# A planner in the kernel sets the order of every engine: chunked attention, then a Fourier mix and an MLP

## The chip, the core and the metric

The kernel runs on one NeuronCore of a Trainium2 chip. The metric is the device time of one execution in microseconds (us). Five engines work side by side and meet through semaphores: PE (TensorE, matrix products, results in PSUM), DVE (VectorE), ACT (ScalarE), POOL (GpSimd) and SP, which only starts DMA transfers. Each engine runs its own list of instructions strictly in the order in which the program put them there: an instruction that has to wait holds up all that stand behind it on its engine. That order is what this change is about.

## What is computed

The reference has two parts. The first is attention in chunks over 4 batches of 8 heads with 768 positions and 64 channels: each chunk of 32 queries sees 8 memory keys, 16 positions to its left, itself and 8 positions to its right.

```
for c in range(nc):
    k_full = np.concatenate([mem_k, k_ctx], axis=2)
    v_full = np.concatenate([mem_v, v_ctx], axis=2)
    scores = scale * np.matmul(q_c, k_full.transpose(0, 1, 3, 2))
    a = np.exp(scores - np.max(scores, axis=-1, keepdims=True))
    a = a / (np.sum(a, axis=-1, keepdims=True) + 1e-09)
    out[:, :, c_start:c_end] = np.matmul(a, v_full)
```

The heads are then laid side by side, so that x has the shape 4 x 768 x 512, and the second part follows (w_ch1 is 512 x 2048, w_ch2 is 2048 x 512):

```
X = np.fft.fft(np.fft.fft(x, axis=1), axis=2)
u = x + np.real(X)
un = (u - mean(u)) / sqrt(var(u) + 1e-6)
out = u + np.maximum(un @ w_ch1, 0.0) @ w_ch2
```

## The kernel before, in words

**Attention** (`emit_keys`, `emit_pair`) works on pairs of heads, four pairs to a batch, 16 in all. For a pair, SP loads q, k and v; the casts of q and k to bf16 (L239, L241) run on DVE for batch 0 and on POOL for the others; POOL copies the overlapping rows of v (L245). PE turns q and k (trq, L250; trk, L259), ACT copies them out of PSUM (qT, L252; kTb, L264). Then there are two groups, each half of the positions: PE computes the scores (sc, L282), ACT the exponential (e, L287), PE the product with v (xa, L299), DVE divides by the sum and writes the activations (L303, L304). There is one PSUM buffer for scores.

**The Fourier mix** (`emit_fx`) of a batch needs all four pairs of it. DVE folds the activations (zy, pq, ff: L319 to L328) for the even part and then for the odd part. ACT rounds the fold to fp16 (hi, L332), DVE takes the rest (lo, L333), PE multiplies both with cosine and sine tables (ps, L341, L348), ACT and DVE split the result again (L355, L356, L358). Six column products follow (pm, L370), one for each tile of 128 positions; DVE adds each to the activations (L379), takes mean and variance (L381, L382) and subtracts the mean (un, L384); PE turns the result (tp, L387) and DVE copies it out (unT, L388). POOL computes the inverse deviation (L391, L392).

**The MLP** (`emit_mlp`) of a batch runs in two halves of 384 positions. A half is 16 groups of 4 matmuls (ph, L403), each followed by a relu on ACT (hT, L406), and then 3 groups of 16 matmuls (pc, L411), each followed by a scaled addition on DVE (osb, L414) and a store. The half's first products need three of the six unT tiles. There are two PSUM buffers for ph and pc together (tag `mlp`), two for the Fourier products (tag `acc`), and one hT.

The tables of cosines and sines are made at the start: DVE computes the angles (L178 to L185), ACT applies Sin (L197 to L203). The weights are loaded by eight transfers that POOL issues (L214, L218).

What sets the order: the scheduler of the framework orders the instructions of each engine, from its own cost model and from priorities. `emit_attention` and `emit_fx` of batch b+1 are emitted before `emit_mlp(b)`, which stands in `tc.high_priority(offset=-100000)`, so that MLP instructions go where the others leave room.

## Time and profile before

| | |
|---|---|
| time before, median of 3 runs | 361.38 us (358.62 to 362.24) |
| the profiled execution | 362.82 us, of which the span from first to last instruction is 360.8 us |
| PE busy | 300.4 us (83% of the span) |
| DVE busy | 196.1 us (54%) |
| ACT busy | 148.6 us (41%) |
| POOL busy | 81.4 us (23%) |

The page cuts the span into 40 equal slices of 9 us and gives for each the busy share of an engine in tenths. Lists of groups give, for one line and kind of instruction, its count, total and mean duration. The timeline gives single instructions with their start and duration; in brackets stands the idle time before and what ended it. A busy PE is not a PE at its peak, since matmuls overlap and their ends are modelled: the throughput is read from long runs of matmuls.

### The profile page before, as it was taken

Reading aid. Unit: us, or ns where it says so; the run is one execution under the profiler, and the core shown is the slowest. Engines: PE = TensorE matmul, PEld = TensorE weight load, DVE = VectorE, ACT = ScalarE, POOL = GpSimd, SP = SyncE. Lnnn points to the kernel's source line nnn. Section 1 sums busy time; section 2 is a strip of 40 time slices with the busy share of each in tenths; the row PEclk is TensorE's granted clock in tenths of the full one; section 3 lists DMA queues with packets and bytes.
Section 4 is the critical chain, followed back from the end, with each engine's and each line's share of the span. In section 5 each row is a group of like instructions: output and inputs, shape, how many; then the busy total and the mean of one; then the engine's idle time right before and its main releaser. Section 6 shows DMA issues by size and latency. Waiting matters only on the chain.

```text
span 360.8 us, 6878 instructions
## 1 busy us (share of the span) xinstructions
PE 300.4 (83%) x2848; PEld 186.3 (52%) x2848; DVE 196.1 (54%) x376; ACT 148.6 (41%) x258; POOL 81.4 (23%) x93
## 2 busy tenths in 40 slices
PE   0225661877899997999999969999999999999995
PEld 0124551656655463666554636775555566554542
DVE  8933339959712139989211398794013987901001
ACT  1654440343372466341743474415651741160530
POOL 7623431601340324020712250206000000100000
PEclk9999985589999999999999998999999999999998
DMA  7997999942000690065402680034101000001001
GB/s 130 200 174 144 189 195 238 156 97 46 6 2 31 146 180 7 32 130 142 133 18 85 161 141 0 2 102 129 25 21 70 0 2 29 37 23 56 34 17 71
DMA packets 42022, 30.65 MB, mean 85 GB/s; under 512 B 30216, under 2 KB 32264, under 8 KB 41992
## 3 DMA queue, kind: packets, MB, share of 16 engines
q1 hardware_dynamic: 35848, 19.73, 29.0%
q0 software_dynamic: 2688, 4.19, 6.6%
q10 hardware_dynamic: 3456, 6.29, 4.7%
q8 instruction: 22, 0.36, 0.5%
q14 instruction: 8, 0.07, 0.1%
HBM read 28.11 MB, written 6.29 MB: 95 GB/s over the span
## 4 chain that ended last, share of the span: by engine, by line
PE 71%; DVE 13%; ACT 8%; issue 3%; POOL 2%; DMA 2%; SPq 1%; ACTq 0%; POOLq 0%; DVEq 0%
PE pc L411 23%; PE ph L403 20%; PE xa L299 9%; PE ps L341 5%; PE pm L370 5%; ACT e L287 3%; PE sc L282 2%; DVE zy L319 2%; ACT hi L332 2%; PE tp L387 2%; PE trq L250 2%; PE trk L259 2%; DMA va<-in_v_dram 2%; DVE pq L322 1%; DVE pq L321 1%
## 5 line engine op out<-in xcount | busy, mean ns | idle before, releaser
L403 PE MATMUL ph<-unT,w_sb 128*128 128x384 f16 x512 | 96.1, 328 | 3.8 <-ACT hT L406 2.9
L411 PE MATMUL pc<-w_sb,hT 128*128 128x512 f16 x384 | 93.1, 380 | 0.0
L406 ACT ACTIVATE hT<-ph 128x384 f16<-128x384 f32 x128 | 61.9, 492 | 71.6 <-PE ph L403 57.7
L403 PEld LDWEIGHTS <-w_sb 128*128 128x128 f16 x512 | 48.1, 98 | 40.7 <-issue 12.6
L411 PEld LDWEIGHTS <-hT 128*128 128x128 f16 x384 | 35.1, 98 | 35.5 <-issue 0.5
L414 DVE SCALAR_TENSOR_TENSOR osb<-pc,rstd,xsb 128x512 f32<-128x512 f32 x24 | 17.9, 746 | 63.7 <-PE pc L411 61.7
L299 PE MATMUL xa<-va,e 128*64 128x65 f32 x768 | 41.6, 253 | 10.2 <-issue 5.3
L299 PEld LDWEIGHTS xa<-va,e 128*64 128x64 f32 x768 | 33.4, 159 | 23.2 <-issue 14.9
L287 ACT ACTIVATE e<-sc,mbias 128x384 f32<-128x384 f32 x64 | 33.7, 579 | 22.1 <-PE sc L282 21.8
L245 POOL COPY va<-va 32x780 f32<-32x780 f32 x32 | 31.0, 986 | 44.8 <-DMA va<-in_v_dram 41.1
L303 DVE RECIPROCAL zs<-xa 128x6 f32<-128x6 f32 x32 | 6.1, 190 | 62.9 <-PE xa L299 62.7
L252 ACT COPY qT<-trq 128x768 bf16<-128x768 bf16 x16 | 12.8, 798 | 51.6 <-PE trq L250 49.9
L239 POOL CAST qb<-qf 96x1024 bf16<-96x1024 f32 x12 | 13.2, 1097 | 83.8 <-PE trq L250 45.2
L341 PE MATMUL ps<-cosS,hi 128*128 128x193 f16 x48 | 11.1, 278 | 14.8 <-ACT hi L332 14.8
L391 POOL TENSOR_SCALAR rstd<-mu_s 128x6 f32<-128x6 f32 x4 | 1.7, 418 | 94.5 <-DVE mu_s L382 69.7
L282 PE MATMUL sc<-qT,kTb 64*128 64x64 bf16 x384 | 12.8, 200 | 9.4 <-ACT e L287 4.7
L332 ACT CAST hi<-ff 128x1536 f16<-128x1536 f32 x8 | 11.8, 1472 | 19.1 <-DVE ff L328 16.0
L341 PEld LDWEIGHTS <-hi 128*128 128x128 f16 x96 | 9.7, 107 | 18.3 <-ACT hi L332 17.9
L264 ACT COPY kTb<-trk 128x832 bf16<-128x832 bf16 x16 | 13.6, 850 | 13.4 <-PE trk L259 13.3
L304 DVE TENSOR_TENSOR xsb<-xa,zs 128x384 f32<-128x384 f32 x32 | 17.7, 554 | 0.8
L282 PEld LDWEIGHTS <-kTb 64*128 64x128 bf16 x384 | 8.9, 99 | 16.8 <-ACT kTb L264 8.6
L355 ACT CAST up<-ps 128x386 f16<-128x386 f32 x16 | 9.6, 599 | 18.0 <-PE ps L341 13.7
(92 smaller groups left out, 381.6 us busy)
## 6 DMA issues: line engine op xcount, KB each, us to landing
qf<-in_q_dram SPq DMA_DIRECT2D x16, 384.0 KB, 3.6
kf<-in_k_dram SPq DMA_DIRECT2D x16, 384.0 KB, 5.2
out_dram<-osb ACTq DMA_DIRECT2D x24, 256.0 KB, 2.0
va<-in_v_dram SPq DMA_DIRECT2D x32, 144.0 KB, 4.1
w_sb<-in_moe_w_ch_dram POOLq DMA_DIRECT2D x8, 512.0 KB, 13.7
va<-in_v_dram SPq DMA_DIRECT2D x32, 48.0 KB, 5.9
va<-in_mem_v_dram SPq DMA_DIRECT2D x32, 24.0 KB
mkf<-in_mem_k_dram SPq DMA_DIRECT2D x1, 64.0 KB
```

Source lines behind the costliest of these rows:

```text
L245: nc.gpsimd.tensor_copy(v1[96:128, 0:NT, 0:D + 1], v1[0:32, 1:NB, 0:D + 1])
L282: nc.tensor.matmul(sc[:, hh, t6, :], kT[r0:r0 + 64, t * BS:t * BS + P], qT[r0:r0 + 64, ts(t, 64)], start=True, stop=True, tile_position=(r ...
L287: nc.scalar.activation(e1[:, :, :, ts(half, 32)], sc[:, :, 0:6, ts(half, 32)], AFT.Exp, bias=mbias[:, half:half + 1], scale=1.0 / math.sqr ...
L299: nc.tensor.matmul(xa[64 * half:64 * half + 64, st, hh, 0:65], e1[:, hh, t6, :], v1[:, 6 * g + t6, 0:65], start=True, stop=True)
L304: nc.vector.tensor_tensor(xb[:, 3 * g:3 * g + 3, h * D:(h + 2) * D].rearrange("p s (h d) -> p s h d", h=2), xa[:, :, :, 0:D], zs.unsqueeze ...
L332: nc.scalar.copy(hi.rearrange(fl), ff.rearrange(fl))
L341: nc.tensor.matmul(ps[:, sp, :], part[:, ab, sp * 3 + st, :], tab[:, sp, st, :], start=(st == 0 and i == 0), stop=(st == 2 and i == 1))
L370: nc.tensor.matmul(pm[:, par, :], lhs, rhs[:, par, :], start=(im == 0), stop=(im == 3))
L403: nc.tensor.matmul(ph[:, 0:384], w1_sb[:, dt, ts(ht, P)], unT[:, dt, sh * 384:(sh + 1) * 384], start=(dt == 0), stop=(dt == NDT - 1))
L406: nc.scalar.activation(hT[:, ht, :], ph[:, 0:384], AFT.Relu)
L411: nc.tensor.matmul(pc, hT[:, ht, ts(stl, P)], w2_sb[:, ht, :], start=(ht == 0), stop=(ht == NHT - 1))
L414: nc.vector.scalar_tensor_tensor(osb, pc, rstd[:, st:st + 1], xb[:, st, :], ALU.mult, ALU.add)
```

## The change

The framework's scheduler is switched off (`tc.manual_schedule()`); the kernel holds a planner, `Plan`, to which every step is added as a task with its engine, a cost in us, the tasks that it needs, the buffers it takes and gives back, and a rank. `Plan.order` goes through time; whenever an engine is idle in the plan, the first task of lowest rank goes next whose needs and buffers are there. The emit functions are then called in the order in which the plan placed them. Attention and the Fourier mix have ranks in the order of the batches, all MLP tasks come behind them (`MLPS`).

Other parts of the change: the four pairs of every batch go in the order 0, 2, 1, 3, and the first fold zy is made in two column halves, the first of which needs only pairs 0 and 2; ff, hi and lo are made in halves; the subtraction of the mean moves from DVE to ACT (`e_un`, with the sign turned, which the relu's `scale=-1.0` turns back); seven clears of buffers move from DVE and POOL to ACT (`e_clear_act`), the clears of kTb from DVE to POOL; Sin moves behind the last exponential of batch 0; the memory keys are loaded on ACT's queue and turned in one matmul; the weights are added once the last exponential of batch 0 is placed; the MLP of the last batch takes a third of its buffers from `acc`.

```diff
-    pair_order = {0: [0, 2, 1, 3]}
+    seq = [(b, pr) for b in range(B) for pr in (0, 2, 1, 3)]
+    plan = Plan(dict(qf=NS, kf=NS, va=NV // 2, kTb=NKT, qb=1, kb=1, qT=2, tr=1, sc=1, xa=1, e1=3,
+                     xsb=3, fold=2, hl=1, up=4, dn=4, acc=2, mlp=2, un=3, unT=2, hT=1, osb=3))
+    add = plan.add
+    MLPS = 1000000
...
+    def order(self):
+        now, idle, wire = 0.0, {}, 0.0
+        waiting = {}
+        for t in self.tasks:
+            waiting.setdefault(t["engine"], []).append(t)
+        for ts_ in waiting.values():
+            ts_.sort(key=lambda t: (t["rank"], t["no"]))
+        gives = []
+        while any(waiting.values()):
...
+            moved = False
+            for e, ts_ in waiting.items():
+                if idle.get(e, 0.0) > now:
+                    continue
+                for t in ts_:
+                    if any(a["done"] is None or a["end" if a["engine"] == e else "done"] > now
+                           for a in t["after"]):
+                        if e == "SP":
+                            break
+                        continue
+                    need = {}
+                    for tag in t["take"]:
+                        need[tag] = need.get(tag, 0) + 1
+                    if any(self.free[tag] < m for tag, m in need.items()):
+                        if e == "SP":
+                            break
+                        continue
+                    for tag in t["take"]:
+                        self.free[tag] -= 1
+                    cost = t["cost"] * (2.0 if e == "PE" and now < 40.0 else 1.0)
+                    idle[e] = t["end"] = now + cost
+                    if t["moved"]:
...
+                        t["done"] = now + cost + self.LAG.get(e, 0.07)
+                    for tag in t["give"]:
+                        gives.append((t["done"], tag))
+                    t["at"] = now
+                    placed.append(t)
+                    ts_.remove(t)
+                    moved = True
+                    break
...
+    def e_clear_act(t):
+        flat = t if len(t.shape) == 2 else t.rearrange("p a b -> p (a b)")
+        nc.scalar.copy(flat, zero[0:flat.shape[0]].to_broadcast(list(flat.shape)))
...
-            zy = fpool.tile([P, NST, HD], FP32, tag="fold", bufs=2, name="zy")
-            nc.vector.tensor_tensor(zy, xb[:, :, 0:HD], xb[:, :, HD:DM], op)
...
-            nc.vector.tensor_scalar(un, xb[:, kt, :], mu_s[:, kt, 0:1], None, ALU.subtract)
...
+    def e_zy(b, par, c):
+        if c == 0:
+            zy_of[b, par] = fpool.tile([P, NST, HD], FP32, tag="fold", bufs=2, name="zy")
+        xb, c0 = xs[b], c * P
+        nc.vector.tensor_tensor(zy_of[b, par][:, :, c0:c0 + P], xb[:, :, c0:c0 + P],
+                                xb[:, :, HD + c0:HD + c0 + P],
+                                ALU.add if par == 0 else ALU.subtract)
...
+    def e_un(b, kt):
+        un_of[b, kt] = un = fpool.tile([P, DM], FP16, tag="un", bufs=3, name="un")
+        nc.scalar.activation(un, xs[b][:, kt, :], AFT.Identity, bias=mu_of[b][:, kt, 0:1],
+                             scale=-1.0)
...
+    def mtag(b, i):
+        return "acc" if b == B - 1 and i % 3 == 2 else "mlp"
...
+        nc.scalar.activation(hT_of[b, sh][:, ht, :], ph_of.pop((b, sh, ht))[:, 0:384], AFT.Relu,
+                             bias=0.0, scale=-1.0)
...
+    t_mkf = add("ACT", 0.2, e_mkf, moved=0.8)
...
+    t_clear["va", 0] = add("ACT", 1.0, lambda: e_clear_act(va[0]), [t_zero])
+    t_clear["va", 1] = add("POOL", 0.9, lambda: nc.gpsimd.memset(va[1], 0.0))
...
+        t_clear["kf", i] = add("ACT", 1.15, lambda i=i: e_clear_act(kf[i]), [t_zero])
+        for m in (2 * i, 2 * i + 1):
+            t_clear["va", m] = add("ACT", 1.0, lambda m=m: e_clear_act(va[m]), [t_zero])
...
+        tq = add("PE", 0.40, lambda: e_turn_q(n), [cq, t_idb], take=("tr",), give=("qb",))
+        eq = add("ACT", 0.80, lambda: e_qT(n), [tq], take=("qT",), give=("tr",))
+        ktag = "acc" if first else "tr"
...
+        for g in range(2):
+            s_ = add("PE", 0.32, lambda g=g: e_scores(n, g), [eq, ek], take=("sc",),
+                     give=("qT", "kTb") if g == 1 else ())
+            x_ = add("ACT", 1.16, lambda g=g: e_exp(n, g), [s_, t_masks], take=("e1",),
+                     give=("sc",))
+            tag = "mlp" if first and g == 1 else "xa"
+            v_ = add("PE", 0.85, lambda g=g: e_values(n, g), [x_] + ov, take=(tag,),
+                     give=("e1", "va") if g == 1 else ("e1",))
+            take = ("xsb",) if g == 0 and n % HP == 0 else ()
+            t_norm[n, g] = add("DVE", 0.78, lambda g=g: e_norm(n, g),
+                               [v_, t_norm[n - n % HP, 0] if (n % HP, g) != (0, 0) else None],
+                               take=take,
+                               give=(tag,))
...
+    t_sines = add("ACT", 6.2, e_all_sines, [t_angle["S"], t_angle["D"], x_last])
+    t_rows = add("DVE", 1.3, e_table_rows, [t_sines])
...
+    t_w1 = [add("POOL", 0.7, lambda dt=dt: nc.gpsimd.dma_start(
+        w1_sb[:, dt, :], moe_w_ch1[ts(dt, P), :]), [x_last], moved=3.5) for dt in range(NDT)]
...
+        for par in range(2):
+            zy[par] = [None]
+            for c in range(2):
+                zy[par].append(add("DVE", 0.96, lambda par=par, c=c: e_zy(b, par, c),
+                                   nrm[c] + [ff, zy[par][-1]],
+                                   take=("fold",) if c == 0 else ()))
...
+            un = add("ACT", 0.72, lambda kt=kt: e_un(b, kt), [sa], take=("un",))
...
+                ph = add("PE", 0.65, lambda sh=sh, ht=ht: e_ch1(b, sh, ht),
+                         mlp_prev + [t_un[3 * sh + i] for i in range(3)] + t_w1,
+                         take=(mtag(b, ht),), give=("unT",) if sh == 1 and ht == NHT - 1 else (),
+                         rank=MLPS + len(plan.tasks))
...
+                    c2 = add("PE", 0.88, lambda sh=sh, stl=stl, part=part: e_ch2(b, sh, stl, part),
+                             [relu[4 * part + 3], t_w2[part], c2], take=(mtag(b, stl),) if part == 0 else (),
+                             give=("hT",) if stl == 2 and end else (),
+                             rank=MLPS + len(plan.tasks))
+                os_ = add("DVE", 0.76, lambda sh=sh, stl=stl: e_osb(b, sh, stl), [c2, rs],
+                          take=("osb",), 
+                          give=(mtag(b, stl), "xsb") if st == NST - 1 else (mtag(b, stl),),
+                          rank=MLPS + len(plan.tasks))
...
-    emit_mem_keys()
-    emit_keys(0)
-    emit_attention(0)
-    emit_fx(0)
-    for b in range(B):
-        if b + 1 < B:
-            emit_attention(b + 1)
-            emit_fx(b + 1)
-        with tc.high_priority(offset=-100000):
-            emit_mlp(b)
+    done = {0: fourier(0)}
+    for b in range(1, B):
+        for i in range(HP):
+            attention(b * HP + i)
+        done[b] = fourier(b)
+    for b in range(B):
+        mlp(b, *done[b])
+    with tc.manual_schedule():
+        for t in plan.order():
+            t["emit"]()
```

ACT at the program's start, before (qT is the copy of the first turned q, e the exponentials of the first group of the first pair):

```order
L252 ACT_TABLE_LOAD
L252 COPY qT<-trq 128x768
L197 ACT_TABLE_LOAD
L197 ACTIVATE sinS<-rS 128x579
L198 ACTIVATE cosS<-yS,hpi_b 128x579
...
L264 COPY kTb_88<-trk 128x13x64
L201 ACTIVATE nsinD<-rD 128x512
L202 ACTIVATE sinD<-rD 128x512
L203 ACTIVATE cosD<-yD,hpi_b 128x512
L287 ACT_TABLE_LOAD
L287 ACTIVATE e_294<-sc,mbias 128x12x32 x2
```

and with the change (va, kf are the buffers of v and k that are cleared; e_620 belongs to the last pair of batch 0):

```order
L227 ACT_TABLE_LOAD
L227 COPY va_82<-zero 128x858
L227 COPY kf_80<-zero 104x1024
...
L227 COPY va_87<-zero 128x858
L291 COPY qT<-trq 128x768
L312 COPY kTb_88<-trk 128x13x64
L331 ACTIVATE e_252<-sc,mbias 128x12x32 x2
...
L331 ACTIVATE e_620<-sc,mbias 128x12x32 x2
L614 ACT_TABLE_LOAD
L614 ACTIVATE sinS<-rS 128x579
```

Seven clears now stand ahead of qT; the seven Sin and two table loads that stood between qT and the first exponential now stand behind the eighth group of exponentials.

DVE at the first Fourier mix, before (xsb holds the activations):

```order
L303 RECIPROCAL zs<-xa 128x6
L304 TENSOR_TENSOR xsb_280<-xa,zs 128x3x128
L319 TENSOR_TENSOR zy<-xsb_280 128x1536
L321 TENSOR_TENSOR pq<-zy 128x768
L322 TENSOR_TENSOR pq<-zy 128x768
...
L319 TENSOR_TENSOR zy<-xsb_280 128x1536
L333 TENSOR_TENSOR lo<-ff,hi 128x1536
```

and with the change:

```order
L371 TENSOR_TENSOR zy<-xsb_297 128x6x128
...
L358 TENSOR_TENSOR xsb_297<-xa,zs 128x3x128
L371 TENSOR_TENSOR zy<-xsb_297 128x6x128
L378 TENSOR_TENSOR pq<-zy 128x768
...
L624 MEMSET nsinD 1x128
...
L401 TENSOR_TENSOR lo<-ff,hi 128x768 x2
L371 TENSOR_TENSOR zy<-xsb_297 128x6x128 x2
```

One half of zy stands before the last pairs' results; eight memsets of the tables (the first is shown) stand ahead of lo.

ACT in the Fourier mix of batch 2, with the change (hT is the relu behind each group of 4 ph, hi and up belong to the mix):

```order
L496 ACTIVATE hT<-ph 128x384
L396 CAST hi<-ff 128x768 x2
L291 COPY qT<-trq 128x768
L496 ACTIVATE hT<-ph 128x384 x2
L312 COPY kTb_88<-trk 128x13x64
L423 CAST up<-ps 128x2x193 x2
L496 ACTIVATE hT<-ph 128x384 x3
L396 CAST hi<-ff 128x768 x2
```

In every mix from batch 1 on, but for the columns of batch 1, groups of the MLP stand between those of the mix. At the program's end 256 ph and 216 pc of PE stand with nothing between them, where before it was 116 and 96.

## Rows read from the trace of the kernel before

**Rows 1.** The page, the span in 40 slices of 9 us.

```profile
PE   0225661877899997999999969999999999999995
...
PEclk9999985589999999999999998999999999999998
DMA  7997999942000690065402680034101000001001
```

**Rows 2.** Timeline of ACT: start us, duration us, line, operation, [idle before].

```profile
22.31 1.05 ACT L287 ACTIVATE e<-sc,mbias 128x384 f32<-128x384 f32 x2
...
51.52 1.05 ACT L287 ACTIVATE e<-sc,mbias 128x384 f32<-128x384 f32 x2 [0.50 <-PE sc L282]
```

**Rows 3.** Windows: us, busy (x instructions) by engine, PEclk, DMA share, GB/s.

```profile
52.57:91.38 38.81, 24.88 (x288) 20.35 (x289) 31.75 (x51) 11.44 (x16) 8.99 (x7) 0.70 0.77 134
91.38:356.60 265.22, 254.49 (x2237) 148.60 (x2236) 135.41 (x244) 114.05 (x208) 47.02 (x47) 0.99 0.25 61
212.00:232.00 20.00, 17.37 (x169) 11.87 (x168) 17.00 (x26) 8.06 (x12) 1.83 (x2) 0.91 0.12 20
252.00:313.00 61.00, 60.03 (x481) 35.11 (x478) 35.37 (x61) 23.28 (x42) 0.83 (x1) 1.00 0.08 26
```

**Rows 4.** Timeline of PE at the start of the MLP and at its end.

```profile
91.38 0.50 PE L403 MATMUL ph<-unT,w_sb 128*128 128x384 f16 x2
...
353.63 2.97 PE L411 MATMUL pc<-w_sb,hT 128*128 128x512 f16 x13
```

**Rows 5.** Groups of DVE by line: total us, mean ns, idle before.

```profile
L101 DVE MEMSET kf<- 104x1024 f32 x3 | 2.7, 912 | 1.3 <-PEq L453 1.0 <-issue 0.3
L179 DVE TENSOR_SCALAR yS<-yS 128x1158 f32<-128x1158 f32 x1 | 1.4, 1446 | 0.0
L183 DVE SCALAR_TENSOR_TENSOR rS<-kk,sv,yS 128x386 f32<-128x386 f32 x3 | 1.7, 603 | 0.0
L185 DVE SCALAR_TENSOR_TENSOR yS<-rS 128x1158 f32<-128x1158 f32 x1 | 1.3, 1347 | 0.0
L103 DVE MEMSET kTb<- 128x624 uint32 x2 | 1.2, 578 | 0.2
```

**Rows 6.** Timeline of DVE: the first k cast.

```profile
14.24 0.71 DVE L241 CAST kb<-kf 104x1024 bf16<-104x1024 f32 x1
```

**Rows 7.** Timeline of PE: one pair's products, early and late.

```profile
38.87 0.87 PE L259 MATMUL trk<-ident_b,kb 104*128 104x104 bf16 x8
...
40.68 0.50 PE L282 MATMUL sc<-qT,kTb 64*128 64x64 bf16 x12 [0.94 <-ACT kTb L264]
...
44.10 2.43 PE L299 MATMUL xa<-va,e 128*64 128x65 f32 x38 [0.79 <-ACT e L287]
...
81.90 0.53 PE L259 MATMUL trk<-ident_b,kb 104*128 104x104 bf16 x8
...
93.33 0.92 PE L299 MATMUL xa<-va,e 128*64 128x65 f32 x24
```

**Rows 8.** Timeline of POOL: the last pair's second overlap copy in batch 0, the weights.

```profile
33.52 0.83 POOL L245 COPY va<-va 32x780 f32<-32x780 f32 x1 [0.99 <-DMA va<-in_v_dram]
34.30 2.41 POOL L214 DMA_DIRECT2D w_sb<-in_moe_w_ch_dram  x4
```

**Rows 9.** The instructions on the weights' tile, last line.

```profile
DMA to landing us min/median/max: 5.3/13.7/24.6
```

**Rows 10.** Groups of DVE by line, Fourier mix.

```profile
L319 DVE TENSOR_TENSOR zy<-xsb 128x1536 f32<-128x1536 f32 x8 | 14.5, 1816 | 0.2
L384 DVE TENSOR_SCALAR un<-xsb,mu_s 128x512 f16<-128x512 f32 x24 | 12.2, 510 | 0.2
L207 DVE MEMSET nsinD<- 1x128 f16 x2 | 0.3, 165 | 0.0
```

**Rows 11.** Timeline of DVE: a fold of 768 columns in the first mix.

```profile
65.89 1.67 DVE L321 TENSOR_TENSOR pq<-zy 128x768 f32<-128x768 f32 x1
```

**Rows 12.** Groups of ACT by line: a table with a bias, 512 columns.

```profile
L203 ACT ACTIVATE cosD<-yD,hpi_b 128x512 f16<-128x512 f32 x1 | 0.7, 706 | 0.0
```

More of the change, by code (lines that the diff above doesn't have):

```diff
@@ L257, in emit_keys @@
             trk = aps.tile([P, RB * KP], BF16, tag="tr", bufs=1, name="trk")
+        tr_of[n, 1] = trk
         for j in range(RB):
@@ L266, in emit_keys, with e_scores @@
-            strided(trk, 0, [[8, NB], [1, 8], [KP, RB]]))
-        qT_of[n], kT_of[n] = qT, kT
-    def emit_pair(n):
+            strided(kTb[n % NKT], 0, [[BS, NB], [8, 8], [1, RB]]),
+            strided(tr_of.pop((n, 1)), 0, [[8, NB], [1, 8], [KP, RB]]))
+    def e_scores(n, g):
+        qT, kT = qT_of[n], kTb[n % NKT]
+        sc_of[n, g] = sc = aps.tile([P, 2, 8, 64], FP32, tag="sc", bufs=1, name="sc")
+        for t6 in range(6):
+            t = 6 * g + t6
+            for hh in range(2):
+                r0 = 64 * hh
+                nc.tensor.matmul(sc[:, hh, t6, :], kT[r0:r0 + 64, t * BS:t * BS + P],
+                                 qT[r0:r0 + 64, ts(t, 64)], start=True, stop=True,
+                                 tile_position=(r0, 0))
@@ new lines, in e_ch2, with e_osb @@
+    def e_ch2(b, sh, stl, part):
+        if part == 0:
+            pc_of[b, sh, stl] = fps.tile([P, DM], FP32, tag=mtag(b, stl), name="pc")
+        for ht in range(4 * part, 4 * part + 4):
+            nc.tensor.matmul(pc_of[b, sh, stl], hT_of[b, sh][:, ht, ts(stl, P)], w2_sb[:, ht, :],
+                             start=(ht == 0), stop=(ht == NHT - 1))
+    def e_osb(b, sh, stl):
+        st = sh * 3 + stl
+        osb_of[b, st] = osb = fpool.tile([P, DM], FP32, tag="osb", bufs=3, name="osb")
+        nc.vector.scalar_tensor_tensor(osb, pc_of.pop((b, sh, stl)), rstd_of[b][:, st:st + 1],
+                                       xs[b][:, st, :], ALU.mult, ALU.add)
@@ new lines @@
+    t_scales = add("DVE", 0.2, e_scales, [t_iota])
+    t_idb = add("DVE", 0.25, lambda: nc.vector.tensor_copy(ident_b, ident), [t_id])
+    t_masks = add("POOL", 0.9, e_masks)
+    for i in range(1, NS):
+        t_clear["kf", i] = add("ACT", 1.15, lambda i=i: e_clear_act(kf[i]), [t_zero])
+        for m in (2 * i, 2 * i + 1):
+            t_clear["va", m] = add("ACT", 1.0, lambda m=m: e_clear_act(va[m]), [t_zero])
+    for i in range(NKT):
+        t_clear["kTb", i] = add("POOL", 1.15, lambda i=i: nc.gpsimd.memset(kTb[i], 0.0))
@@ new lines, with e_mps @@
+    t_mkb = add("DVE", 0.22, lambda: nc.vector.tensor_copy(
+        mkb, mkf.rearrange("p h d -> p (h d)")), [t_mkf])
+    mps_of = []
+    def e_mps():
+        mps_of.append(aps.tile([P, P], BF16, tag="xa", bufs=1, name="mps"))
+        nc.tensor.transpose(mps_of[0], mkb, ident_b)
+    t_mps = add("PE", 0.1, e_mps, [t_mkb, t_idb], take=("xa",))
+    t_mkT = add("DVE", 0.22, lambda: nc.vector.tensor_copy(
+        mkT.rearrange("p a m -> p (a m)"), mps_of[0]), [t_mps], give=("xa",))
+    x_last = [attention(n) for n in range(HP)][-1]
```

628 lines of the change are left out of this document (367 added, 261 removed).

## The prediction

> **What bounds the kernel now.** I read the page's slices first [rows 1]. PE is nearly full from slice 10 (about 90 us) to the end; before that it has digits between 0 and 8, while the transfers have their nines there. So the program has two parts: a start of 91 us, in which PE waits for others, and a stretch from the first matmul of the MLP at 91.38 to the end of the last at 353.63 + 2.97 = 356.60 [rows 4], 265.2 us, in which PE is busy for 254.5 [rows 3] and sets the time. Another 4.2 us to the end of the span (360.8) are the last osb and its store.
>
> The start has two stages. In the first, the four pairs of batch 0 go through a chain of ACT and PE: ACT applies Sin first, so the first exponential runs only at 22.31, and the last ends at 51.52 + 1.05 = 52.57 [rows 2]. The second is the first Fourier mix, 52.57 to 91.38, 38.8 us, with DVE busy for 31.8 of them and PE for 24.9 [rows 3]: DVE's chain sets it. In the long stretch PE loses 10.7 us: 2.6 of them in 212 to 232, around a mix, where also the granted clock is 0.91, but only 1.0 in the 61 us after 252 [rows 3].
>
> **First stage: to the last exponential of batch 0.** Sin and its two table loads leave the path. What then holds the first exponential is k: its cast ends at 14.24 + 0.71 = 14.95 [rows 6] because DVE is full ahead of it. Of that work two kf clears (0.91 each), two kTb clears (0.58 each), L179 (1.45), three L183 (0.60 each) and L185 (1.35) [rows 5] now stand behind the cast or on another engine: 1.8 + 1.2 + 1.4 + 1.8 + 1.3 = 7.5 us. About 1 us comes ahead (angles of the second table), so the cast ends near 8.4. The seven clears on ACT cost about what an ACT instruction of that length does (0.71 for 512 columns [rows 12], so 1 us, 7 us in all, as an estimate) and end near 9, beside this. Then trk 0.87, the copy of k about 0.9, sc 0.50 [rows 7]: first exponential at 10.7.
>
> From there one pair takes, in the new order of PE (sc, xa, sc, xa, with the next pair's trq and trk between): twice sc 0.50, e 1.05 and xa 24/38 of 2.43 = 1.53 [rows 2, 7], together 6.2; of trq and trk (1.7 together, trq taken like trk) 1.05 lies beside an exponential, 0.65 doesn't; six handovers of some 0.06 add 0.4. That makes 7.2 us; before, three and a half pairs lay between 22.31 and 51.52 [rows 2], 8.3 for one. Four pairs, less the last xa, end at 10.7 + 4 x 7.2 - 1.5 = 38. So this stage gives 52.6 - 38 = **14.6 us**. Bounds: the second copy of the last pair's v ends at 33.52 + 0.83 = 34.35 after a wait for transfers [rows 8], and sc of that pair's second group stands behind xa of its first; with transfers just as early as now, xa could not start before 34.4, and the exponential would end at 37; a stream without the dip to 7 in slice 3 [rows 1] could give 33. Above, 8.3 us for each pair gives 42. I take 38, from the rows of the pair itself.
>
> **Second stage: the first mix.** Off DVE's chain go half of one zy (0.91; it runs before the last pairs) and three un of 0.51 ahead of the first ph [rows 10], 2.4 us. On ACT an un costs about 0.71, read from a table with a bias of the same 512 columns [rows 12]; it runs beside the next tile's DVE work, so nothing is added. Halves of ff, hi and lo let PE and ACT start earlier; DVE's idle time in the stage is 38.8 - 31.8 = 7.0 us [rows 3], and I let it fall by 2.4. Added: eight memsets of 0.165 [rows 10] = 1.3 us, now between ff and lo, and about 0.8 for more and shorter instructions. 38.8 - 2.4 - 2.4 + 1.3 + 0.8 = **36**, so the first ph comes at 74. Bounds: 32 (all DVE idle time gone) to 40 (Sin, seven instructions and two table loads, is late for the first ps: then ps waits with hi, which stands behind Sin on ACT).
>
> The weights must have landed by then. They go out at 34.30 now [rows 8] and land 5.3 to 24.6 us after issue [rows 9]. In the new order they stand on POOL behind the q cast of pair 5, which needs PE to have turned q of pair 4, about 36 here; an issue at 37 to 43 lands by 68 at the latest. The cover is 6 us.
>
> **The long stretch.** PE's list is the same but for what it does before the first ph: two xa groups, two sc groups, two trq and one trk more than before (xa 0.92, trk 0.53, trq like trk, sc at most 0.50 [rows 7]), 4 us in all. PE's losses there are the 10.7 us idle and 1.8 for the dip (0.09 of 20 us is lost clock) [rows 3]; a greedy order in which MLP groups stand between the groups of the mixes should take back about half, so 6; bounds 0 and 10. For the third PSUM buffer of the last MLP nothing is counted: PE is full there with two (nines in the last slices [rows 1]). 265.2 - 4 - 6 = **255**.
>
> **Sum.** 38 + 36 + 255 + 4.2 = 333 us of span. The profiled execution took 362.82, 2.0 more than its span, and is 1.4 above the median of the runs: 333 + 2.0 - 1.4 = **334 us**.
>
> **Rule against row, the clock.** The duration of one trk falls from 0.87 at 38.87 to 0.53 at 81.90 [rows 7], though the clock's digits show 9 in the first slices and a drop only in 7 and 8 [rows 1]; for the early pairs I go by durations, those of the low level. The Trainium skill (TensorE: Matmul & The Clock Gate, Part 1) says that PE starts at 1.2 GHz and that sustained work releases 2.4 GHz; the later rows agree, the digits of the first slices don't. By that rule the denser pairs of the new order would run fast before the last of them, and the sum would be that of the first rival instead of 334.
>
> **Rivals.**
>
> *The clock rises within the first pairs.* trk falls from 0.87 to 0.53 and xa from 1.53 to 0.92 [rows 7], trq like trk: two xa, trk and trq make 1.9 us a pair, 4 us from the third pair on, capped at 33 to 37 by the transfers. The mix's first ps run faster too, 1 to 2 us on DVE's chain, and with the best of the stretch (10 instead of 6) it is 334 - 8 to 10: **325**. For it: PE works for 5.8 of each pair's 7.2 us. Against it: in the old order the low rate lasts past 40 us (sc 0.50 at 40.68 [rows 7]).
>
> *The start gives less:* weights or v land late, since batch 1's loads share the transfers with them (DMA stays at 7 to 9 through slice 7 [rows 1]). An issue at 50 instead of 37 to 43 and the longest landing put the first ph at 85: **345**. For it: the cover is only 6 us and the queue on POOL is strictly in order.
>
> *Slower than before.* PE waits at the head of its list. In a mix PE has work for 24.9 of 38.8 us even with attention beside it [rows 3]; if the planned order brings no MLP groups into those gaps, three later mixes lose 13.9 each, 42 instead of 10.7: 31 more than now, and nothing of the 6 comes back: 334 + 37 = **371**. It decides where DVE runs later than planned by more than the few MLP groups between two groups of the mix can cover. It can: a fold of 768 columns took 1.67 us [rows 11] where one of 1536 takes 1.82 [rows 10]. The Trainium skill (SBUF — State Buffer, Who interferes with whom) has DVE instructions with two SBUF inputs contend with POOL's reads; no run here separates that from other delays. Against it: in the new order MLP groups stand between most groups of the mixes, and the fill before (61 us with 1.0 lost) was also a fixed list.
>
> *The change doesn't do what it says:* the orders come out as good as the old one outside the start, and the start is held by transfers: 355 to 361, no change within 1%.
>
> **Chances.** Forecast 0.55 (its own range 327 to 341), clock 0.17 (319 to 327), less at the start 0.15 (341 to 353), no change 0.05, slower 0.08. Range for 8 in 10: 319 to 350. A measurement of this kernel tells about 1% from no change. Faster by more: 0.55 + 0.17 + 0.15 = 0.87; within 1%: 0.05; slower: 0.08.
>
> **What would show it.** Right: on ACT's timeline the first exponential at 10 to 12 and the eighth group's end at 36 to 40; the first ph at 70 to 78; from there to the last pc 250 to 260; no PE digit under 9 in the last 90 us but the last. Wrong: a first ph after 82 (look at what ended PE's wait: the weights, or DVE), trk at 0.53 by the third pair (the clock), or more than 15 us of PE idle time between the first ph and the pure MLP, with ps, pm or tp waiting for DVE or ACT.

## The result, and the profile after

The changed kernel takes 345.55 us (median of 4 runs, 343.32 to 351.67) where the kernel before takes 360.79 on the same chip: ratio 0.956, interval 0.948 to 0.964. Forecast were 334 us, range 319 to 350. The execution of 351.67 us was a slow one and is not in the ratio. The profiled execution took 344.71 us; its span is 342.6.

The slices of the page after (40 of 8.6 us; they answer to [rows 1]):

```profile
PE   0678647959998886859999998699999999999995
...
DVE  6954497958079999799793459860720100101001
...
PEclk9999999969999999998999999699999999999999
```

PE has work from the second slice on, but digits of 5 to 8 also stand in slices 12 to 17 (103 to 154 us), where before there were mostly nines. ACT's timeline (answers to [rows 2]): the first and the eighth group of exponentials, and Sin behind it.

```profile
12.29 1.05 ACT L331 ACTIVATE e<-sc,mbias 128x384 f32<-128x384 f32 x2 [0.60 <-PE sc L323]
...
37.76 1.05 ACT L331 ACTIVATE e<-sc,mbias 128x384 f32<-128x384 f32 x2 [1.47 <-PE sc L323]
38.83 1.28 ACT L614 ACT_TABLE_LOAD   x1
```

Windows after (columns as in [rows 3]): first mix; first ph to last pm; from there to the last pc, which is all MLP but for three tp (called the pure MLP here).

```profile
38.81:77.98 39.17, 25.43 (x349) 20.95 (x349) 30.68 (x63) 25.46 (x40) 19.95 (x19) 0.92 1.12 196
...
77.98:243.73 165.75, 149.82 (x1641) 100.29 (x1640) 121.06 (x214) 88.81 (x159) 41.61 (x40) 0.97 0.34 73
243.73:338.48 94.75, 94.36 (x504) 48.27 (x501) 13.95 (x23) 31.98 (x67) 1.59 (x2) 1.00 0.10 40
```

So the first stage ends at 38.81 (before 52.57), the first mix takes 39.2 us (before 38.8), and from the first ph to the last pc it is 260.5 (before 265.2). The tail is 4.1. But for 0.4 us, PE's idle time in the long stretch lies ahead of the pure MLP: 165.75 - 149.82 = 15.9 us.

Two places show what fixed lists do. In the first mix PE stands 3.73 us for a cast that POOL makes late, since q of pair 7 (pairs are numbered from 0) has not landed; behind that trq stand tp, unT and the first ph. POOL's and PE's timelines:

```profile
72.49 1.03 POOL L272 CAST qb<-qf 96x1024 bf16<-96x1024 f32 x1 [3.45 <-DMA qf<-in_q_dram]
```
```profile
69.47 0.38 PE L468 MATMUL tp<-ident_h,un 128*128 128x128 f16 x4 [0.17 <-DVE xsb L449]
73.58 0.82 PE L286 MATMUL trq<-ident_b,qb 96*128 96x96 bf16 x8 [3.73 <-POOL qb L272]
...
77.55 0.63 PE L468 MATMUL tp<-ident_h,un 128*128 128x128 f16 x4
77.98 1.02 PE L489 MATMUL ph<-unT,w_sb 128*128 128x384 f16 x4
78.93 0.92 PE L347 MATMUL xa<-va,e 128*64 128x65 f32 x24
```

The pause costs more than its 3.73 us: behind it PE works at the durations of its low level (four tp take 0.63 instead of 0.38) until 78.9, where xa takes 0.92 again.

A little later DVE waits 8.5 us for xa of pair 7, which stands on PE behind ten ph groups (86.73 to 93.68); from 97.6 to 139 DVE then has no gap over 0.41 us, and PE waits for it in turn:

```profile
94.65 0.20 DVE L357 RECIPROCAL zs<-xa 128x6 f32<-128x6 f32 x1 [8.51 <-PE xa L347]
```
```profile
86.73 7.02 PE L489 MATMUL ph<-unT,w_sb 128*128 128x384 f16 x40 [0.21 <-ACT hT L496]
93.68 0.92 PE L347 MATMUL xa<-va,e 128*64 128x65 f32 x24
```

### The profile page after: what moved, and what is told of

Same layout as the page of the kernel before. It is cut to its first block, busy times and chain, and to the rows that moved or that the text cites. A ratio compares the mean times of both kernels' runs of the same rounds, so it can differ in the third digit from the quotient of the medians.

```text
span 342.6 us, 6911 instructions
## 1 busy us (share of the span) xinstructions
PE 292.4 (85%) x2833; PEld 188.3 (55%) x2833; DVE 190.6 (56%) x374; ACT 168.9 (49%) x297; POOL 82.2 (24%) x89
## 4 chain that ended last, share of the span: by engine, by line
PE 63%; DVE 16%; DMA 8%; SPq 3%; ACT 3%; issue 3%; POOL 3%; ACTq 0%; POOLq 0%
PE ph L489 23%; PE pc L503 22%; PE xa L347 6%; DMA qf<-in_q_dram 5%; PE pm L443 5%; PE ps L411 4%; DMA kf<-in_k_dram 2%; SPq L259 2%; DVE lo L401 2%; DVE zy L371 1%; PE tp L468 1%; DVE pq L379 1%; ACT e L331 1%; PE sc L323 1%; DVE xsb L358 1%
## 5 line engine op out<-in xcount | busy, mean ns | idle before, releaser
L489 PE MATMUL ph<-unT,w_sb 128*128 128x384 f16 x512 | 91.2, 326 | 1.4 <-ACT hT L496 0.8
L503 PE MATMUL pc<-w_sb,hT 128*128 128x512 f16 x384 | 88.3, 381 | 0.0
L280 POOL COPY va<-va 32x780 f32<-32x780 f32 x32 | 37.4, 1177 | 48.3 <-DMA va<-in_v_dram 40.8
L347 PE MATMUL xa<-va,e 128*64 128x65 f32 x768 | 34.6, 250 | 7.9 <-ACT e L331 3.7
L461 ACT ACTIVATE un<-xsb,mu_s 128x512 f16<-128x512 f32 x24 | 17.3, 722 | 22.4 <-DVE mu_s L456 22.3
L411 PE MATMUL ps<-cosS,hi 128*128 128x193 f16 (+1 forms) x72 | 16.8, 284 | 3.2 <-DVE ff L388 3.2
L411 PE MATMUL ps<-cosS,lo 128*128 128x193 f16 (+1 forms) x72 | 16.5, 284 | 3.1 <-DVE lo L401 3.1
L449 DVE TENSOR_TENSOR xsb<-pm,xsb 128x512 f32<-128x512 f32 x24 | 16.3, 678 | 4.1 <-PE pm L443 3.9
L401 DVE TENSOR_TENSOR lo<-ff,hi 128x768 f16<-128x768 f32 x16 | 17.3, 1103 | 1.5 <-ACT hi L396 1.4
L396 ACT CAST hi<-ff 128x768 f16<-128x768 f32 x16 | 13.1, 832 | 9.8 <-DVE ff L388 9.7
```

The lines of the kernel that those rows point to most:

```text
L280: nc.gpsimd.tensor_copy(v1[96:128, 0:NT, 0:D + 1], v1[0:32, 1:NB, 0:D + 1])
L347: nc.tensor.matmul(xa[64 * half:64 * half + 64, st, hh, 0:65], e1[:, hh, t6, :], v1[:, 6 * g + t6, 0:65], start=True, stop=True)
L401: nc.vector.tensor_tensor(lo[:, ab].rearrange(fl), ff_of[b, par][:, ab].rearrange(fl), hi[:, ab].rearrange(fl), ALU.subtract)
L411: nc.tensor.matmul(out_[:, sp, :], part[:, ab, sp * 3 + st, c0:c1], tab[:, sp, st, :], start=(st == 0 and i == 0), stop=(st == 2 and i == 1))
L461: nc.scalar.activation(un, xs[b][:, kt, :], AFT.Identity, bias=mu_of[b][:, kt, 0:1], scale=-1.0)
L489: nc.tensor.matmul(ph[:, 0:384], w1_sb[:, dt, ts(ht, P)], unT_of[b][:, dt, sh * 384:(sh + 1) * 384], start=(dt == 0), stop=(dt == NDT - 1))
```

## The experiments

Ratios are to the kernel before, from runs on the same chip as each kernel, with 95% intervals. `shift(a, b)` takes step a of the planned list and puts it at place b.

**1. Pair 7 earlier.** 317 and 325 are POOL's overlap copies of pair 7, 329 and 336 PE's two xa.

```diff
+        shift(317, 284); shift(325, 285); shift(329, 308); shift(336, 315)
```

> The changed kernel's planned order, but pair 7 of batch 1 (numbered from 0) is served earlier: POOL makes its two overlap copies ahead of rstd, and PE computes its two xa behind the 6th and the 9th ph group instead of behind all 16. Theory DVE-chain: in the changed kernel DVE waits 8.5 us (86.1 to 94.6) for that xa, is then full without a gap from 97.6 to 139, and PE loses 10.7 us between 98 and 158 to that. Then DVE's wait falls to under 2 us, the fold of batch 1 starts 6 to 7 us earlier, PE's idle time between 98 and 158 falls from 10.7 to 4 to 6, and the time is 4 to 6 us under the changed kernel's 345.6: ratio to the kernel before 0.940 to 0.945. Rival handovers: the idle time of PE comes from short waits between the engines in a fixed order, and an earlier fold only makes DVE idle later: 0 to 1 us less, ratio 0.953 to 0.956.

Measured: ratio 0.9536 (0.947 to 0.960), the rival's side. The fold of batch 1 did come earlier (pq 14.1 us behind the first ph, at 94.69 - 80.64, instead of 98.62 - 77.98 = 20.6), but then DVE reached its next step in the list, an osb that needs a pc behind the ph groups:

```profile
94.69 0.96 DVE L378 TENSOR_TENSOR pq<-zy 128x768 f32<-128x768 f32 x1
95.56 0.95 DVE L379 TENSOR_TENSOR pq<-zy 128x768 f32<-128x768 f32 x1
102.21 0.75 DVE L509 SCALAR_TENSOR_TENSOR osb<-pc,rstd,xsb 128x512 f32<-128x512 f32 x1 [5.69 <-PE pc L503]
```

The wait of 8.5 us became 1.8 + 2.2 + 5.7, and PE's idle time between 98 and 158 us is 10.0 instead of 10.7. (This profiled execution took 349.3 us, 3.2 above its kernel's median.) Here one step moved in a fixed list met the next.

**2. trq of pair 7 later.**

```diff
+        shift(249, 261)   # behind sc(6, 1), tp(0, 1), tp(0, 2), pm(0, 4)
```

> The changed kernel's planned order with one step moved: PE turns q of pair 7 behind sc(6,1), tp(0,1), tp(0,2) and pm(0,4) instead of ahead of them. Theory head of line: the 3.7 us that PE stood before trq at 73.58 held up tp, and with it unT and the first ph (78.0). Then the first ph comes at 74 to 75, and the time is 3 to 4 us under the changed kernel's 345.6: ratio 0.945 to 0.949. Rival transfers: what is late is the data of pairs 6 and 7; the first ph comes earlier, but PE and DVE wait as long for xa, trk and trq of these pairs a few us later, and the time stays within 1 us of the changed kernel's: ratio 0.954 to 0.958.

Measured: 0.9568 (0.951 to 0.962), while its own stage did what was expected: the mix takes 36.3 us (39.92 to 76.26), the predicted 36. PE's wait is 0.42 instead of 3.73:

```profile
75.68 0.52 PE L286 MATMUL trq<-ident_b,qb 96*128 96x96 bf16 x8 [0.42 <-POOL qb L272]
76.03 0.39 PE L468 MATMUL tp<-ident_h,un 128*128 128x128 f16 x4
76.26 0.81 PE L489 MATMUL ph<-unT,w_sb 128*128 128x384 f16 x4
```

From there to the last pm it takes 168.7 us instead of 165.75: the gain is lost later. It is not lost in the waits that the rival names: PE's idle time there is 16.4 us instead of 15.9, its busy time 152.3 instead of 149.8, with a granted clock of 0.95 instead of 0.97.

**3. The second weight matrix later.**

```diff
+        for i in (155, 156, 157, 157):  # its four transfers, behind the k cast of pair 6
+            shift(i, 191)
```

> The changed kernel's planned order, but POOL starts the four transfers of the second weight matrix (2.1 of 4.2 MB) behind the k cast of pair 6, at 55 to 64 us, instead of directly behind those of the first at 43.7 to 46.7. Theory transfers: the weights slow the loads of v of pair 6 and of q and k of pair 7 (the issues of v took 3.5 and 7.0 us there instead of 0.3 and 0.5), and this holds PE at trq. Then q of pair 7 lands 4 to 8 us earlier (cast at 64 to 68 instead of 72.5), PE's 3.7 us before trq are gone, the first ph comes at 73 to 75, the first pc still finds its weights, and the time is 3 to 5 us under 345.6: ratio 0.942 to 0.949. Rival: the bytes only change places; loads of pairs 8 and 9 or the first pc (94.5) wait instead: ratio 0.955 to 0.965.

Measured: 0.9589 (0.954 to 0.964). The transfers theory holds for the load (the cast runs at 68.11 and PE's wait is gone) but not for the time: the first ph still comes at 77.98. The eighth group ended 1.4 us later in this execution (40.22), and the mix takes 37.8 us, of which DVE is busy for 33.9 instead of 30.7. Part of that comes from the edit: POOL's cast and copies, which no longer stand behind the transfers, ran at 45.03 and 46.28, beside one of DVE's folds, and that pq took 2.36 us (at 44.58) instead of 0.95.

**4. Sin among the first pairs.**

```diff
+        shift(143, 77)    # the seven Sin, behind e(0, 1) and qT(1)
```

> The changed kernel's planned order, but the seven Sin stand among the first pairs again (behind e(0,1) and qT(1)) instead of behind the eighth group of exponentials. Theory start: the first stage is a chain of ACT and PE, so the Sin (5.6 us from 38.83 with the table load) and another table load of 1.3 for the exponentials lengthen it: eighth group's end at 45 to 46 instead of 38.8; the mix gets back about 1 us, since kT of pair 4 and hi no longer stand behind Sin. Time 4 to 6 us above 345.6: ratio 0.967 to 0.974. Rival: the first stage is held by transfers (busy share 9 tenths from slice 1 on), which go on under the Sin, so that later pairs catch up: 0 to 2 us above, ratio 0.956 to 0.962.

Measured: 0.9593 (0.953 to 0.965), within the interval of the changed kernel. The eighth group ends at 39.60, not at 45, 0.8 us later than in the changed kernel. But the 0.8 us are not the price of Sin: the third group of exponentials starts 4.0 us later (24.49 instead of 20.51) and the fifth still 3.5 (30.96 instead of 27.43). Then, in this execution, PE went over to 2.4 GHz in the third pair, and three groups later the delay was down to 0.8:

```profile
30.96 1.05 ACT L331 ACTIVATE e<-sc,mbias 128x384 f32<-128x384 f32 x2 [2.16 <-PE sc L323]
```
```profile
33.28 0.35 PE L323 MATMUL sc<-qT,kTb 64*128 64x64 bf16 x12
...
37.24 0.92 PE L347 MATMUL xa<-va,e 128*64 128x65 f32 x24 [0.76 <-ACT e L331]
```

**5. The kernel before, Sin late.** Its scheduler is kept; the Sin get a bias made from the last exponential (the angles of the first table stay in the fold's buffers until then; those of the second get a buffer of their own).

```diff
+            if n == 3 and g == 1:
+                nc.vector.tensor_scalar(late[:, 0:1], e1[:, 1, 5, 63:64], 0.0, 0.0, ALU.mult, ALU.add)
+                nc.vector.tensor_scalar(late[:, 1:2], e1[:, 1, 5, 63:64], 0.0, math.pi / 2.0, ALU.mult, ALU.add)
...
-            nc.scalar.activation(sinS[:, par], r[:, :, par], AFT.Sin, bias=0.0, scale=scS)
+            nc.scalar.activation(sinS[:, par], rS[:, :, par], AFT.Sin, bias=late[:, 0:1], scale=scS)
```

> The kernel before, its orders still from the framework's scheduler, with one part of the change: the seven Sin wait for the last exponential of batch 0 (their bias is a tile that two tiny DVE instructions make from it), and the angles of the second table get buffers of their own. Theory Sin: Sin ahead of the first exponential was the largest loss of the start, and the first stage is a chain of ACT and PE. Then the first exponential comes at about 16.5 (k's cast ends at 14.95) instead of 22.3, the eighth group ends at 46 to 47 instead of 52.6, the mix behind it is 0 to 1 us longer, and the ratio to the kernel before is 0.983 to 0.987. Rival order: what shortened the start in the changed kernel is the planner's order of the casts, the clears and PE's products (with it, Sin among the first pairs left the eighth group's end at 39.6 against 38.8); then the eighth group ends at 50 or later and the ratio is 0.993 to 1.003.

Measured: 0.9963 (0.994 to 0.999), and the eighth group ends at 49.62: the rival's numbers. But the edit brought two delays of its own. The angles of the second table now stand ahead of k's cast on DVE (four instructions, 2.3 us together), so the cast runs at 16.55 instead of 14.24. And the memsets of the tables, which wait for Sin, stand on DVE ahead of the last pair's activations: DVE waited 4.56 us there (until 54.42), and the mix takes 41.3 us instead of 38.8. So the first exponential moves from 22.31 to 19.70 only.

What Sin cost can be read from the kernel before itself. PE's first trk and first sc there, ACT's copy of k, and the first trk in this experiment's kernel and in the changed one:

```profile
15.01 0.87 PE L259 MATMUL trk<-ident_b,kb 104*128 104x104 bf16 x8 [2.85 <-DVE va L109]
17.69 0.50 PE L282 MATMUL sc<-qT,kTb 64*128 64x64 bf16 x12 [1.80 <-ACT kTb L264]
```
```profile
16.80 0.83 ACT L264 COPY kTb<-trk 128x832 bf16<-128x832 bf16 x1
```
```profile
17.28 0.87 PE L267 MATMUL trk<-ident_b,kb 104*128 104x104 bf16 x8 [4.91 <-DVE va L109]
```
```profile
9.87 0.88 PE L302 MATMUL trk<-ident_b,kb 104*128 104x104 bf16 x8 [0.60 <-DVE kb L276]
```

Before, the first scores were ready at 18.19, but ACT had three Sin and a table load to do before the exponential at 22.31: 4.1 us. The copy of k had waited 0.9 behind the four Sin ahead of it (trk ended at 15.88). So Sin held the first exponential for 5.0 us. k's cast ends 5.1 us earlier in the changed kernel (9.81 instead of 14.95). Together that is 10.1 of the 10.0 us by which the first exponential came earlier; and 5.0 less the 2.3 of the later cast is 2.7, where this experiment measured 2.6. The other 3.7 of the 13.8 us lie between the first exponential and the end of the eighth group, in the length of a pair.

PE's timeline of one pair in this kernel and of one in the changed kernel, both at the low level:

```profile
36.09 0.88 PE L267 MATMUL trk<-ident_b,kb 104*128 104x104 bf16 x8
37.91 0.50 PE L290 MATMUL sc<-qT,kTb 64*128 64x64 bf16 x12 [0.94 <-ACT kTb L272]
39.61 0.50 PE L290 MATMUL sc<-qT,kTb 64*128 64x64 bf16 x12 [1.21 <-ACT e L295]
40.05 0.48 PE L312 MATMUL xa<-va,e 128*64 128x65 f32 x4
41.32 2.43 PE L312 MATMUL xa<-va,e 128*64 128x65 f32 x38 [0.79 <-ACT e L295]
43.75 0.82 PE L258 MATMUL trq<-ident_b,qb 96*128 96x96 bf16 x8
```
```profile
23.62 0.50 PE L323 MATMUL sc<-qT,kTb 64*128 64x64 bf16 x12
25.33 1.57 PE L347 MATMUL xa<-va,e 128*64 128x65 f32 x24 [1.21 <-ACT e L331]
26.83 0.50 PE L323 MATMUL sc<-qT,kTb 64*128 64x64 bf16 x12
27.26 0.82 PE L286 MATMUL trq<-ident_b,qb 96*128 96x96 bf16 x8
28.43 0.87 PE L302 MATMUL trk<-ident_b,kb 104*128 104x104 bf16 x8 [0.35 <-DVE kb L276]
29.23 1.57 PE L347 MATMUL xa<-va,e 128*64 128x65 f32 x24
```

Before, both xa stand behind both sc, and the next pair's turns behind those: 36.09 to 45.08, 9.0 us for a pair. With the change the turns stand between e and xa: sc 23.62 to sc 30.73, 7.1 us.

**6. un on DVE, and 7. with it zy whole and two PSUM banks** (lists as planned for the change).

```diff
-        nc.scalar.activation(un, xs[b][:, kt, :], AFT.Identity, bias=mu_of[b][:, kt, 0:1], scale=-1.0)
+        nc.vector.tensor_scalar(un, xs[b][:, kt, :], mu_of[b][:, kt, 0:1], -1.0, ALU.subtract, ALU.mult)
```

> The changed kernel and its planned order; only the subtraction of the mean (un) runs on DVE again, at its place of the planned list (tensor_scalar with subtract and a multiplication by -1). Theory un: DVE is full from 97 to 139 us and gets 6 x 0.51 = 3.1 us more there, 1.5 us more ahead of the first ph, while the mixes that have MLP groups beside them hide it: 3 to 5 us above the changed kernel's 345.6, ratio 0.964 to 0.971. Rival: the handover from DVE to ACT and the 0.72 us there cost the chain of one tile as much as 0.51 on DVE gives, so nothing changes: ratio 0.954 to 0.960.

> The changed kernel's planned order with three other parts of the change undone together: un on DVE, zy in one instruction of 1536 columns at the place of its second half, and the MLP of the last batch in two PSUM banks. Theory order: the planned orders and the start carry the gain, and these parts are worth what un alone is worth (the prediction put 0.9 us on half a zy in the first mix and nothing on the third bank): ratio 0.964 to 0.973, not more than 1 us above the kernel with un alone undone. Rival parts: each of them holds a chain that sets the time; a late zy delays the first ps of all four mixes by 0.95 us, and two banks bring waits into the pure MLP at the end (94.4 of 94.75 us busy with three): ratio 0.975 to 0.985.

Measured: un alone 0.9604 (0.957 to 0.964), between the two theories, all three 0.988 (0.984 to 0.992), on the rival's side and above its range. With un on DVE the first ph comes at 77.95, no later than in the changed kernel; the cost lies behind it. Windows of both, un alone first: the stretch behind the second mix's first ps, and the pure MLP.

```profile
104.85:155.11 50.26, 39.26 (x581) 28.88 (x580) 45.46 (x84) 27.65 (x49) 24.35 (x23) 0.97 0.75 150
...
247.15:342.23 95.08, 94.55 (x504) 48.18 (x501) 14.98 (x26) 30.34 (x64) 1.59 (x2) 1.00 0.10 39
```
```profile
103.72:159.40 55.68, 42.92 (x581) 31.79 (x581) 47.23 (x83) 28.61 (x50) 28.82 (x24) 0.88 0.68 137
...
250.82:351.24 100.42, 96.62 (x504) 48.06 (x501) 14.97 (x26) 30.88 (x64) 1.59 (x2) 1.00 0.10 37
```

Some 5.4 us come from each. In the second kernel, lists planned for three banks run in two.

**8. Two banks, planned so.**

```diff
-        return "acc" if b == B - 1 and i % 3 == 2 else "mlp"
+        return "mlp"
```

> The changed kernel with the MLP of the last batch in two PSUM banks, in the plan too. Theory of the prediction (a third bank is worth nothing, since PE is full with two): from the last pm to the last pc 94.8 to 96 us instead of 94.75, ratio as of the changed kernel, 0.953 to 0.960. Rival: with three parts undone together this stretch took 100.4 us, so the third bank is worth 5 us there: 99 to 101 us, ratio 0.968 to 0.974.

Measured: 0.9539 (0.951 to 0.957); the pure MLP takes 96.60 us instead of 94.75. The third bank is worth 1.9 us there; most of the 5 in the kernel with three parts undone was the list that did not fit.

**9. PE kept busy.**

```diff
+        def keep_busy(count):
+            for _ in range(count):
+                nc.tensor.matmul(idle, ident_b, ident_b, start=True, stop=True)
...
+        if n < HP:
+            keep_busy(8)
...
+        if (n, g) == (HP - 1, 1):
+            keep_busy(40)
```

> The changed kernel with matmuls that serve nothing, into unused columns of the scores' buffer: 8 (128 x 128, bf16) ahead of each xa of batch 0, where PE waits 0.4 to 1.2 us for the exponential, and 40 behind the last xa of batch 0, where PE waits 6.4 us for kT. Theory clock: PE stays at 1.2 GHz until 52 us (xa 1.57, sc 0.50) because it pauses; without pauses it reaches 2.4 GHz (xa 0.92, sc 0.35) by the third pair and keeps it in the first mix. Then the eighth group of exponentials ends at 34 to 37 instead of 38.8, the first ph comes at 71 to 75, and the ratio is 0.943 to 0.951. Rival: the first stage waits for transfers and ACT, and more work on PE is answered by a lower granted clock behind the rise: eighth group 37 to 41, first ph 76 to 79, ratio 0.954 to 0.962.

Measured: 0.947 (0.943 to 0.951), the theory's ratio; but eighth group 39.11 and first ph 79.06, the rival's numbers. The stages of this execution (345.96 us, 1.6 above its kernel's median) don't show where the ratio comes from, its interval meets that of the changed kernel, and so neither side is shown. The added matmuls (L341) waited for the exponential too, so they filled no pause and stood in PE's way, 1.0 us a group at first. But the level rose at 24.7 us and held to the end of the pairs:

```profile
24.70 1.20 PE L355 MATMUL xa<-va,e 128*64 128x65 f32 x24
25.84 0.35 PE L323 MATMUL sc<-qT,kTb 64*128 64x64 bf16 x12
27.39 0.61 PE L341 MATMUL sc<-ident_b 128*128 128x128 bf16 x8 [1.21 <-ACT e L331]
27.93 0.92 PE L355 MATMUL xa<-va,e 128*64 128x65 f32 x24
```

A pair then takes 5.9 us (sc 25.84 to sc 31.72) with two such extras in it. A way to fill the pauses themselves was not tried.

**10 and 11. Other costs in the planner.** Nothing but costs differs; the second is the same with three steps and 46.0 instead of 52.0.

```diff
-                    cost = t["cost"] * (2.0 if e == "PE" and now < 40.0 else 1.0)
+                    cost = t["cost"] * (2.0 if e == "PE" and now < 52.0 else 1.0)
...
+    SCALE = {'e_scores': 1.17, 'e_sum': 1.1, 'e_values': 0.85, 'e_qT': 0.93, 'e_rows': 1.18, 'e_hi': 1.18, ...
+    for t in plan.tasks:
+        f = t["emit"]
+        names = [x for x in f.__code__.co_freevars + f.__code__.co_names if x.startswith("e_")]
+        t["cost"] *= SCALE.get((names or [f.__name__])[0], 1.0)
+        t["moved"] *= dict(POOL=0.85, SP=1.07).get(t["engine"], 1.0)
```

> The changed kernel with other costs in its planner, nothing else: 17 steps scaled by 0.85 to 1.39 (among them lo 1.39, stats 1.18, hi 1.18, ps 1.18, xa 0.85), weights 0.85, loads 1.07, PE counted double until 52 us instead of 40. The costs were picked so that the lists, replayed with durations of the changed kernel's trace, leave PE 5 us of idle time between the first ph and the last pm instead of 16. Theory order: that idle time comes from lists that do not fit the chip, so a list that fits gets half or more of it back: idle time 6 to 10 us instead of 15.9, 6 to 10 us less time, ratio to the kernel before 0.930 to 0.942. Rival: the waits only move, since DVE runs slower beside POOL than the replay has it and the granted clock falls wherever PE pauses: idle time 13 to 18 us, ratio 0.950 to 0.960.

> The changed kernel with other costs in its planner: osb and the columns times 1.18, up times 1.08, weights 0.85, loads 1.08, PE counted double until 46 us. Replayed with durations of the changed kernel's trace, its lists leave PE 8 us of idle time between the first ph and the last pm. Theory order: idle time 8 to 12 us instead of 15.9, 4 to 8 us less time, ratio 0.935 to 0.946. Rival, the waits only move: idle time 13 to 18 us, ratio 0.950 to 0.960.

Measured: **0.9017 (0.899 to 0.904), 327.3 us**, and 0.9221 (0.919 to 0.926), with 7.6 and 8.2 us of idle time between the first ph and the last pm, as their theories had it; both ratios are lower than the theories said. The first kernel's windows: first mix, first ph to last pm, pure MLP.

```profile
38.34:74.27 35.93, 24.46 (x333) 20.72 (x333) 31.16 (x59) 25.25 (x40) 17.90 (x18) 0.77 1.10 208
...
74.27:226.06 151.79, 144.22 (x1669) 96.98 (x1667) 121.38 (x220) 87.84 (x161) 45.35 (x42) 1.00 0.37 83
226.06:320.59 94.53, 94.15 (x500) 48.06 (x497) 13.09 (x21) 31.80 (x66) 1.59 (x2) 1.00 0.10 40
```

Between first ph and last pm it needs 14.0 us less than the changed kernel: idle time 7.6 instead of 15.9, so 8.3 less, and 5.6 less of busy time, with the granted clock at 1.00 instead of 0.97. So less idle time went with less busy time for about the same matmuls, as behind the pause at 73.58 above.

**12. Measured costs in the planner.**

```diff
+    COST = {'e_pq': 1.9, 'e_lo': 0.92, 'e_zy': 0.92, 'e_values': 0.85, 'e_ch1': 0.68, 'e_overlap': 0.87, ...
```

> The changed kernel with mean durations from its own trace as the planner's costs for 30 kinds of steps (pq 1.9, lo 0.92, zy 0.92, xa 0.85, ph 0.68, overlap copy 0.87 and so on), nothing else. It asks whether wrong costs or the draw of a greedy order left PE 15.9 us of idle time between the first ph and the last pm. Theory costs: a plan made with true durations fits the chip; idle time 6 to 10 us, ratio 0.930 to 0.945. Rival draw: most costs were within 0.1 us already, and which of two ready steps a greedy order takes first decides; replayed, these lists gain 3 us and not the 14 of the picked ones: idle time 12 to 16 us, ratio 0.945 to 0.957.

Measured: 0.9534 (0.948 to 0.959), idle time 12.9 us (in an execution of 341.3 us, 4.0 below its kernel's median):

```profile
78.24:240.33 162.09, 149.18 (x1641) 100.31 (x1639) 116.16 (x212) 88.83 (x160) 45.22 (x42) 0.96 0.37 73
```

The rival: truer costs alone don't make the list better. The replay had put these lists 3 us under the changed kernel's and the picked ones of experiment 10 some 14; by the ratios, measured are 1 and 20. Both kernels whose lists were picked by a replay gained, the one with lists that were not picked did not; more than these three were not run.

## Why the prediction was right, and where it failed

The time fell in the range, but not in the forecast's own part of it (327 to 341). It lies where the rival with less gain at the start had it (341 to 353), and not by that rival's mechanism: the first ph came at 77.98, not at 85, and nothing waited for the weights. (That rival's sum doesn't come out either: an issue at 50 and the longest landing of 24.6 us give 74.6.) The 12 us above the forecast are +0.8 in the first stage, +3.2 in the mix, +5.5 in the stretch, +2 from the profiled execution, which here lies 0.8 below its median instead of 1.4 above.

- **First stage (38 predicted, 38.81).** The size is right, the cost of a pair too (7.2, measured 7.1), and so is the mechanism: of the 13.8 us, Sin on the path is 5.0, k's cast 5.1 and the shorter pairs 3.7 (experiment 5; in the changed kernel all four pairs ran at the low level, so a risen clock is no part of it). Two errors of size cancel: the cast ended at 9.81 and not at 8.4, the first exponential came at 12.29 and not at 10.7, and from there to the end of the eighth group it took 26.5 us and not 27.3. Sin put back among the first pairs cost 3.5 to 4.0 us until the clock rose (experiment 4); this and the late Sin of experiment 5 agree with a share of some 3.5 to 5 us.
- **First mix (36 predicted, 39.2).** The step that failed is the 2.4 of DVE's idle time that the halves were to give back: DVE's idle time rose to 8.5 us (39.17 - 30.68) from 7.1, and PE's 3.7 us behind one late cast are most of the miss. With that trq moved the mix takes 36.3, with the better lists of experiment 10 35.9. No ph waited for the weights, though they landed 8.6 to 29.4 us after issue, so some after 70 us and not by 68; that they slow the loads of pairs 6 and 7 I had only as a risk for the first ph itself. The three un that were to give 1.5 us ahead of the first ph show no gain there (experiment 6).
- **The long stretch (255 predicted, 260.5).** "A greedy order should take back about half, so 6" failed: PE's idle time is 16.3 us there (260.50 - 244.19) instead of 10.7, 15.9 of it ahead of the pure MLP, with ps waiting for DVE in 5.7 of them: the prediction's own sign of being wrong. That the stretch still came out 5.5 and not some 12 us too long is luck: PE's busy time fell by 10.3 instead of the 4 counted, 6.8 of it in xa (25.2 us for 528 matmuls before, 18.4 for 480 after), for which the runs show no cause. The same planner with other costs gives 246.3, and with truer ones the whole gains nothing clear of the noise, so neither the planner's rule nor its costs' truth decides, but which list came out.
- **The third bank at nothing**: 1.9 us by experiment 8. **un on ACT**, for which the long stretch counted nothing: it takes 722 ns, as predicted, and back on DVE the stretch takes 264.3 us instead of 260.5.
- **The rivals.** The clock rival did not come in the profiled execution (trk 0.88 at 37.59), but it is near: with the same list the level rose at 32 us in one execution and after 47 in others. The reading of the clock's digits in the prediction is off by one: counted from 0 as elsewhere there, the fall to 5 stands in slices 6 and 7, with 8 beside it. The slower rival's mechanism, PE at the head of its list, is what the idle time shows, at a sixth of the price it had (5.6 us more than before instead of 31).

## What to carry to other kernels

Moving single steps of a list fixed in advance gained nothing here in three tries: the wait went to the next step (1), the gain was lost in slower matmuls (2), or the move set POOL's work beside DVE's (3). Re-planning the whole list gained, so re-plan, and again whenever a buffer or an engine changes (experiments 7 and 8). Judge candidate lists by replaying them with durations from a trace, and look at idle time of the engine that sets the end; a greedy plan is one draw, and here draws lay some 20 us apart (ratios 0.902 to 0.956). A stage that is shortened by itself need not shorten the whole: the first mix lost 2.9 us in experiment 2 and the time stayed. And an edit that is to test one step can bring delays of its own, so read the timelines of the other engines too before the ratio is taken for an answer.
